# Head loads of a fused S5 and feed-forward kernel: equal halves on both queues, x cut by columns over all rows

## The chip, the cores and the metric

The kernel runs on one core of one Trainium2 chip. The metric is the device time of one execution in microseconds, the median of several runs. The engines of the core are TensorE (PE; its weight loads are PEld), VectorE (DVE), ScalarE (ACT), GpSimd (POOL) and SyncE (SP). SP and ACT issue DMAs, each on a queue of its own, and sixteen DMA engines serve both queues.

## The reference

One input x of shape [1, 2048, 448] in bfloat16 goes through two branches, which a gate mixes.

```python
x = A_x
g = _sigmoid((x * gate_w).sum(-1, keepdims=True))
a = _A_ref(x, Lambda_re, Lambda_im, B_re, B_im, C_re, C_im, log_dt, Dskip)
b = _B_ref(x, B_w1, B_w2)
return g * a + (1 - g) * b
```

Branch A is a diagonal complex state space: `Bu = x @ B_bar.T`, `h[t] = Lam_bar * h[t-1] + Bu[t]` over 2048 steps, `y = 2 * Re(h @ C.T) + x * Dskip`, with `dt = exp(log_dt)`, `Lam_bar = exp(dt * Lam)` and `B_bar = (Lam_bar - 1) / Lam * B`. Branch B is `silu(x @ w1) @ w2` with 1792 hidden columns. The input that B has under the name `B_x` isn't used: both branches take `A_x`.

## The kernel before

**Tiling.** Two successive time steps stand in one row: `x2` is [1024, 896], and columns 0-447 of it are the even steps, 448-895 the odd ones. TensorE needs x with its features on the partitions: `XT[:, j, :]` holds features 128j to 128j+127 of the even steps for j = 0 to 3, and of the odd steps for j = 4 to 7. The 448 features make three full row blocks and a remainder of 64 (j = 3), which shares TensorE with another remainder, one on the lower and one on the upper 64 partitions. `XR` holds the remainder on the other half of the partitions. `W1E[:, j, :]` is w1 in the same row blocks, its 1792 hidden columns cut into 14 blocks of 128, called fb.

**The order.** The program is written out by hand. A small tracker (class `Tracker`) turns the keys that each operation reads and writes into semaphore waits; the order on an engine is the order of the Python calls. An engine takes its instructions in that order, so what stands behind a waiting one waits too. The DMA issues of the ACT queue stand between ACT's own instructions.

**The head** is all that stands ahead of the first full feed-forward pair:

- Loads. The first 512 rows of `x2`, columns 0-511, come into `XH` as they are, in four row blocks k of 128 rows (SBUF partition p, block k). The first 768 columns of w1 come in row blocks j = 0, 1, 2. `XA` names the keys of the pieces of x. Before, SP loads: columns 0-255 of x block 0, half of the columns of W1 block 0, columns 0-383 of x block 2, all of W1 block 1, two small rows into `R` (log_dt and Lambda_re), columns 384-511 of x blocks 2 and 3. ACT loads: columns 0-255 of x block 1, the other half of W1 block 0, columns 0-383 of x block 3, columns 256-511 of x blocks 0 and 1, the row Lambda_im, all of W1 block 2. Behind these come, on both queues, the remainder of w1 (`ld_wr`) and the later columns (`ld_w3`). SP waits for the first remainder loads (`T.wait_all("sp", gE)`) ahead of its DMA transposes, which bring the rest of x, B and C.
- Transposes on TensorE. `turn_k(j, k)` (line 488) transposes a 128 x 128 block of `XH` into a PSUM bank; `turned_k` (line 498, 128 columns) and `turned_x` (line 504, 256 or 512 columns) copy it with VectorE into `XT`. `PB` gives the bank for each j.
- `ffn1_first` (line 430) is a generator: 24 matmuls for six hidden blocks over the first 512 rows, 12 for j = 0 with the rows in two halves h of 256 columns, then 6 each for j = 1 and j = 2 with 512 columns. `next(first)` runs it to its next `yield`, and transposes, copies and small work stand between.
- `rd` (line 463, VectorE) and `mm_cols` (line 469, TensorE) turn the three rows in `R` into columns (`PV`), from which VectorE and ACT make dt, the decay and the phases.
- `turned_x(3)` and the copy at line 568 write the remainder of x to `XT` and `XR`. `ffn1_rem` (line 444) adds the remainder matmuls, and the SiLU on ACT (line 452) empties two banks at a time. `warm` (line 478) issues matmuls on constants, the first 20 of them while the first loads are under way.

Behind the head the matmuls of line 362 (`lanes`) run, first the rest of the feed-forward for these 512 rows, then the others, the state space's `Bu`, the second feed-forward matmul (lines 811 and 796) and the output (line 1049).

Of the kernel before, what the change touches and what calls it, by code (L numbers as in the profile page):

```python
# [11 lines left out]
BF16 = DT.bfloat16  # L12
# [138 lines left out]
def gated_mix(nc, A_x, A_Lambda_re, A_Lambda_im, A_B_re, A_B_im, A_C_re, A_C_im, A_log_dt,  # L151
              A_Dskip, B_x, B_w1, B_w2, gate_w, out):
    with ExitStack() as ctx:
        E = ctx.enter_context
        T = Tracker(nc, ctx)

        def sb(name, shape, dtype):
            return E(nc.sbuf_tensor(name, list(shape), dtype))
# [4 lines left out]
        XT = sb("XT", [128, 8, NK], BF16)  # L163
        W1E = sb("W1E", [128, 4, F_FF], BF16)
# [6 lines left out]
        XR = sb("XR", [128, NK], BF16)  # L171
# [17 lines left out]
        ID = sb("ID", [128, 128], BF16)  # L189
# [31 lines left out]
        ps = E(nc.psum_tensor("ps", [128, 8, 512], F32))  # L221
# [3 lines left out]
        def ld(eng, dst, src, key, group=None):  # L225
            return T.dma(eng, lambda e: e.dma_start(dst, src), writes=[key], group=group)  # L226
# [5 lines left out]
        XE = [(["XTe000", "XTe001", "XTe010", "XTe011", "XTe02"], ["XTe03"]), (["XTe1"], ["XTer1"])]  # L232
        XO = [([f"XTo{h}"], [f"XTr{h}"]) for h in range(2)]

        def swap_xr(eng, h, odd):
# [18 lines left out]
        XA = ["XA0", "XA1", "XA2", "XA3", "XB0", "XB1"]  # L254
        FA, FB = 768, 1280
        x0 = x2[0:512, 0:512].rearrange("(k p) c -> p k c", p=128)

        def ld_w(eng, j, f0=0, f1=FA, key=""):
            ld(eng, W1E[:, j, f0:f1], B_w1[j * 128:(j + 1) * 128, f0:f1], f"W1Ej{j}{key}")

        def ld_row(eng, i, v):
            ld(eng, R[i:i + 1, 0:D], row(v), f"R{i}", gR if i < 2 else gR2)
# [9 lines left out]
                          B_w1[384:448, FA:].rearrange("p (n c f) -> p n c f", n=2, c=2)[:, :, c, :], f"W1Es{c}")  # L272
            return ld(eng, W1E[p, 3, 0:384], B_w1[384:448, 384 * c:384 * c + 384], f"W1Er{c}")

        for k, eng in enumerate(("sp", "act")):
            ld(eng, XH[:, k, 0:256], x0[:, k, 0:256], XA[k])
        for c, eng in enumerate(("sp", "act")):
            ld_w(eng, 0, 384 * c, 384 * c + 384, c)
        for k, eng in ((2, "sp"), (3, "act")):
            ld(eng, XH[:, k, 0:384], x0[:, k, 0:384], XA[k])  # L280
        ld_w("sp", 1)
        ld("act", XH[:, 0:2, 256:512], x0[:, 0:2, 256:512], XA[4])
        for i, (eng, v) in enumerate((("sp", A_log_dt), ("sp", A_Lambda_re), ("act", A_Lambda_im))):
            ld_row(eng, i, v)
        ld_w("act", 2)
        ld("sp", XH[:, 2:4, 384:512], x0[:, 2:4, 384:512], XA[5])
        T.op("act", lambda e: e.activation(JK[:, 0:1], HP[:, :], AF.Exp), reads=["HP"], writes=["JK0"])
        gE = [ld_wr(eng, c, False) for c, eng in enumerate(("sp", "act"))]
        ld_w3("sp", 0, 2, FA, FB, "d")
# [20 lines left out]
        for i, src in enumerate((A_B_re, A_B_im)):  # L310
# [15 lines left out]
             writes=["IOTA"])  # L326
# [9 lines left out]
        def nxt():  # L336
            n_bank[0] += 1
            return BANKS[(n_bank[0] - 1) % len(BANKS)]
# [58 lines left out]
        def ff(fb):  # L397
            i, c = fb // 2, fb % 2
            return i + 3 * c if i < 3 else i + 3 + 2 * c if i < 5 else i + 5 + 2 * c

        def wj(fb):
            i, c = fb // 2, fb % 2
            return [f"W1Ej0{c}", "W1Ej1", "W1Ej2"] if i < 3 else ["W1Ed0", "W1Ed2"] if i < 5 else ["W1Ee0", "W1Ee1"]
# [13 lines left out]
        def ffn1_pair(c, fb, p=None):  # L417
            odd, h = c // 2, c % 2
            banks = at(p) if p is not None else [nxt(), nxt()]
            return (*[(banks[i], odd, h, w1(fb + i)) for i in range(2)],  # L420
                    wj(fb) + wj(fb + 1) + (XO if odd else XE)[h][0], rem_ffn1(odd, h, fb),
                    lambda: ffn1_act(c, fb, banks[0], 2))

        def ffn1_first():
            banks = [nxt() for _ in range(NF1)]
            for j, h in ((0, 0), (0, 1), (1, None), (2, None)):
                c = slice(0, 512) if h is None else slice(256 * h, 256 * h + 256)
                for n, fb in enumerate((0, 2, 4, 1, 3, 5)):
                    bank = banks[fb]
                    T.op("pe", lambda pe, fb=fb, bank=bank, j=j, h=h, c=c: pe.matmul(  # L430
                        ps[:, bank, c], W1E[:, j, ff(fb) * 128:(ff(fb) + 1) * 128], XT[:, j, c],
                        start=(h == 0), stop=(h == 0), skip_group_check=(h != 0)),
                        reads=[f"W1Ej{j}" if j else f"W1Ej0{fb % 2}"] + (
                            ["XTe02"] if j == 2 else [f"XTe0{j}{h}"] if h is not None else [f"XTe0{j}0", f"XTe0{j}1"]),
                        writes=[f"ps{bank}"])
                    if (j, h, n) in ((0, 0, 3), (0, 0, 5), (1, None, 2), (1, None, 5)):
                        yield
            yield banks

# [34 lines left out]
        def warm(n, b):  # L474
            def mm(pe):
                ins = None
                for _ in range(n):
                    ins = pe.matmul(ps[:, b, 0:128], ones, ones, start=True, stop=True)
                return ins
            T.op("pe", mm, writes=[f"ps{b}"])  # L480

        warm(NWARM, 5)
        PB = (6, 7, 6, 7)
        xp = [ps[:, b, 0:256].bitcast(BF16) for b in PB]

        def turn_k(j, k, b=None):
            b = PB[j] if b is None else b
            T.op("pe", lambda pe: pe.transpose(  # L488
                ps[:, b, 0:256].bitcast(BF16)[:, k * 128:(k + 1) * 128], XH[:, k, j * 128:(j + 1) * 128], ID[:, :]),
                reads=[XA[k if j < 2 or (j == 2 and k > 1) else 4 + k // 2], "ID"], writes=[f"ps{b}"])  # L490

        def turn_x(j, i):
            for k in (2 * i, 2 * i + 1):
                turn_k(j, k)

        def turned_k(j, k, b):
            c = slice(128 * k, 128 * k + 128)
            T.op("dve", lambda e: e.tensor_copy(XT[:, j, c], ps[:, b, 0:256].bitcast(BF16)[:, c]),
                 reads=[f"ps{b}"], writes=[f"XTe0{j}{k // 2}" + ("" if k % 2 else "a")])

        def turned_x(j, i=None, b=None):
            c, key = (slice(0, 512), f"XTe0{j}") if i is None else (slice(256 * i, 256 * i + 256), f"XTe0{j}{i}")
            b = PB[j] if b is None else b
            T.op("dve", lambda e: e.tensor_copy(XT[:, j, c], ps[:, b, 0:256].bitcast(BF16)[:, c]),
                 reads=[f"ps{b}"], writes=[key])

        for k in range(2):
            turn_k(0, k, 6 - k)
            turned_k(0, k, 6 - k)
        turn_x(1, 0)  # L510
        turned_x(1, 0)
        warm(2, 4)
        first = ffn1_first()
        next(first)
        for k in (2, 3):
            turn_k(0, k, k + 4)
            turned_k(0, k, k + 4)
# [12 lines left out]
        turned_x(2)  # L530
        next(first)
        for i in range(2):
            turn_x(3, i)
# [24 lines left out]
        def pact(o, a, f, ra, scale=1.0, bias=0.0):  # L558
# [9 lines left out]
        T.op("dve", lambda e: e.tensor_copy(XR[64:128, 0:512], xp[3][0:64, :]), reads=["ps7"], writes=["XR0a"])  # L568
        T.op("act", lambda e: e.activation(JK[:, 0:1], HP[:, :], AF.Silu), reads=["HP"], writes=["JK0"])
        ld_b(GWB, gate_w, "GW")  # L570
        ld_b(DB, A_Dskip, "DB")
# [9 lines left out]
            reads=["f2"] + SGN, writes=["f2s"])  # L581
# [84 lines left out]
        for n in (32, 64):  # L666
            T.op("dve", lambda e, n=n: e.tensor_copy(GD[n:2 * n, :, :], GD[0:n, :, :]), reads=["GW", "DB"],
                 writes=["GW", "DB"])
# [7 lines left out]
             writes=["BTz"] + BTK[2:4])  # L676
# [174 lines left out]
        def bu_even(pt, h, p=None, q=None):  # L851
# [4 lines left out]
            def done():  # L856
# [14 lines left out]
        def bu3_even(p, q):  # L871
            b = at(p)

            def done():
# [288 lines left out]
        f = ffn1(2)  # L1163
# [100 lines left out]
```

## Time and profile before

| What | us |
|---|---|
| Median of 3 runs | 137.05 (136.32 to 137.05) |
| Span of the profiled execution | 135.2 |
| PE busy | 131.8 (97%) |
| DVE busy | 115.6 (86%) |
| ACT busy | 93.8 (69%) |
| POOL busy | 15.9 (12%) |

The span runs from the first instruction of the profiled execution to its last; a run's time holds what lies around it too. PE counts matmuls, PEld weight loads, which overlap them. The chain of waits follows the work that ended last back from its end, so its shares tell who sets the time. In a timeline or chain line the first number is the start and the second the length, both in us; what stands in brackets is the idle time of the engine ahead of it and who ended it. Two groups of the page show what the DMA queues carry in all (packets, MB, share of 16 engines): `q1` is SP's queue, `q10` ACT's.

```
q1 hardware_dynamic: 22996, 10.43, 33.4%
q10 hardware_dynamic: 1730, 1.20, 3.1%
```

### The profile page before, as it was taken

How to read it: one execution, taken by the hardware profiler on the slowest of the kernel's cores; microseconds unless marked ns; L12 is line 12 of the kernel's file. 1: busy time of each engine (PE TensorE's matmuls, PEld its weight loads, DVE VectorE, ACT ScalarE, POOL GpSimd, SP SyncE). 2: the span in 40 equal slices, each digit the busy share in tenths (PEclk: the TensorE clock that was granted, in tenths of full speed). 3: DMA queues.
4: the chain of work that ended last, by engine and by line, in shares of the span. 5: the costliest groups of instructions: out<-in, count | busy, mean ns of one | idle time of the engine just before them, and what ended most of it. 6: DMA issues, size and time to landing. Idle time of an engine off the chain costs nothing.

```text
span 135.2 us, 2632 instructions
## 1 busy us (share of the span) xinstructions
PE 131.8 (97%) x1072; PEld 65.4 (48%) x1073; DVE 115.6 (86%) x154; ACT 93.8 (69%) x146; POOL 15.9 (12%) x32
## 2 busy tenths in 40 slices
PE   7899999999999999999999999999999999999993
PEld 7444444444444554444445544445555555555552
DVE  1369999917899798999999999999999999994554
ACT  0459888899939999769999597797114437879200
POOL 7108349650000000000000000000000000000000
DMA  4999979898997220000222000000000000322123
GB/s 110 259 275 176 125 140 264 165 323 248 259 188 119 53 63 0 0 0 0 55 47 58 5 0 0 0 5 0 0 0 0 0 0 5 102 91 79 68 80 124
DMA packets 24736, 11.78 MB, mean 87 GB/s; under 512 B 16851, under 2 KB 24214, under 8 KB 24726
## 3 DMA queue, kind: packets, MB, share of 16 engines
q1 hardware_dynamic: 22996, 10.43, 33.4%
q10 hardware_dynamic: 1730, 1.20, 3.1%
q8 instruction: 8, 0.13, 0.4%
q14 instruction: 2, 0.02, 0.0%
HBM read 5.34 MB, written 1.84 MB: 53 GB/s over the span
## 4 chain that ended last, share of the span: by engine, by line
PE 94%; DMA 2%; DVE 1%; SPq 1%; issue 0%
PE ps L362 44%; PE ps L796 16%; PE ps L811 16%; PE ps L1049 15%; PE ps L430 3%; DMA XN<-in_A_x_dram 2%; PE ps L488 1%; DVE TMPS L1073 1%; SPq L226 1%; PE ps L444 1%; PE ps L469 0%
## 5 line engine op out<-in xcount | busy, mean ns | idle before, releaser
L362 PE MATMUL ps<-XT,W1E 64*128 64x512 bf16 x325 | 41.3, 376 | 0.0
L452 ACT ACTIVATE AT<-ps 128x1024 bf16<-128x1024 f32 x28 | 28.2, 1020 | 7.4 <-PE ps L362 7.2
L362 PEld LDWEIGHTS ps<-XT,W1E 64*128 64x128 bf16 x325 | 16.9, 94 | 19.1 <-ACT AT L452 0.3
L362 PE MATMUL ps<-XT,BT 64*128 64x512 bf16 x156 | 22.4, 376 | 0.0
L811 PE MATMUL ps<-W,AT 64*128 64x448 bf16 x224 | 21.5, 349 | 0.0
L796 PE MATMUL ps<-W,AT 128*128 128x448 bf16 x112 | 21.4, 353 | 0.0
L796 PEld LDWEIGHTS ps<-W,AT 128*128 128x128 bf16 x112 | 10.9, 98 | 10.5 <-issue 0.4
L811 PEld LDWEIGHTS ps<-W,AT 64*128 64x128 bf16 x224 | 10.9, 94 | 10.4
L840 ACT ACTIVATE BT<-ps,GT 128x448 bf16<-128x448 f32 x8 | 5.1, 634 | 13.2 <-PE ps L796 13.2
L896 DVE SCALAR_TENSOR_TENSOR HS<-VE,P,ps 128x512 bf16<-128x512 bf16 (+1 forms) x13 | 9.6, 781 | 3.8 <-PE ps L362 3.8
L362 PEld LDWEIGHTS ps<-XT,BT 64*128 64x128 bf16 x156 | 8.1, 94 | 9.4 <-DVE HS L896 0.4
L940 DVE TENSOR_TENSOR_SCAN G<-P,Q 128x1024 f32<-128x1024 f32 (+1 forms) x6 | 11.4, 1922 | 0.0
L1049 PE MATMUL ps<-CO,VE 128*128 128x448 bf16 (+2 forms) x63 | 11.1, 332 | 0.0
L1049 PE MATMUL ps<-CO,HS 128*128 128x448 bf16 x56 | 11.1, 352 | 0.0
L362 PE MATMUL ps<-XR,W1E 64*128 64x512 bf16 x25 | 9.2, 376 | 0.0
L1049 PEld LDWEIGHTS ps<-CO,VE 128*128 128x128 bf16 x63 | 6.0, 98 | 4.8
L1049 PEld LDWEIGHTS ps<-CO,HS 128*128 128x128 bf16 x56 | 5.5, 98 | 5.1
L893 DVE TENSOR_TENSOR Q<-G,COS 128x2048 bf16<-128x2048 f32 (+1 forms) x4 | 7.0, 1756 | 0.1
L893 DVE TENSOR_TENSOR Q<-G,SIN 128x2048 bf16<-128x2048 f32 (+1 forms) x4 | 7.0, 1752 | 0.0
L858 ACT ACTIVATE VE<-ps 128x1024 bf16<-128x1024 f32 x6 | 6.1, 1020 | 1.2 <-PE ps L362 1.2
L860 ACT ACTIVATE ps<-VE,P 128x1024 f32<-128x1024 bf16 x6 | 6.7, 1118 | 0.2
L896 DVE SCALAR_TENSOR_TENSOR VE<-HS,P,FP 128x512 bf16<-128x512 bf16 (+1 forms) x7 | 6.6, 977 | 0.1
(124 smaller groups left out, 181.0 us busy)
## 6 DMA issues: line engine op xcount, KB each, us to landing
W<-in_B_w_dram SPq DMA_DIRECT2D x2, 784.0 KB, 6.3
XN<-in_A_x_dram SPq DMA_DIRECT2D x1, 896.0 KB, 5.5
out_dram<-OT SPq DMA_DIRECT2D x8, 112.0 KB, 1.7
out_dram<-TMPS SPq DMA_DIRECT2D x7, 112.0 KB, 1.7
HS<-HS SPq DMA_DIRECT2D x4, 128.0 KB, 2.3
XN<-in_A_x_dram SPq DMA_DIRECT2D x1, 384.0 KB, 3.6
W1E<-in_B_w_dram SPq DMA_DIRECT2D x1, 256.0 KB, 5.6
W1E<-in_B_w_dram ACTq DMA_DIRECT2D x1, 256.0 KB, 5.6
```

Source lines behind the costliest of these rows:

```text
L362: ins = pe.matmul(ps[:, bank, :], w(p, j), xh(odd, h, j, p), start=start and j == js[0], stop=stop and j == js[-1], skip_group_check=seeded)
L430: T.op("pe", lambda pe, fb=fb, bank=bank, j=j, h=h, c=c: pe.matmul(ps[:, bank, c], W1E[:, j, ff(fb) * 128:(ff(fb) + 1) * 128], XT[:, j, c] ...
L452: T.op("act", lambda e: e.activation(a[:, fb:fb + n, :], ps[:, bank:bank + n, :], AF.Silu), reads=[f"ps{bank + i}" for i in range(n)], wri ...
L796: ins = pe.matmul(ps[:, bank, 0:D], a[:, fb, q * 128:(q + 1) * 128], W2[:, ff(fb), :], start=(first and fb == 0), stop=(fb == NFB - 1), sk ...
L811: ins = pe.matmul(ps[:, bank, 0:D], a[p, fb, q * 128:(q + 1) * 128], W2[p, ff(fb), :], start=(start and fb == 0), stop=(not start and fb = ...
L840: T.op("act", lambda e: e.activation(bs(tile), ps[:, bank, 0:D], AF.Copy, scale=sc), reads=[f"ps{bank}", "GT2" if h else "GRI"], writes=ks)
L858: T.op("act", lambda e: e.activation(VE[:, m:m + 2, hs], ps[:, b[0]:b[0] + 2, :], AF.Copy), reads=[f"ps{i}" for i in b], writes=vs)
L860: T.op("act", lambda e: e.activation(ps[:, o[0]:o[0] + 2, :], VE[:, m:m + 2, hs], AF.Copy, scale=c1("lr", pt)), reads=vs + ["lr"], writes= ...
L893: T.op("dve", lambda e: e.tensor_tensor(o, a, b, op), reads=reads, writes=writes)
L896: T.op("dve", lambda e: e.scalar_tensor_tensor(o, a, s, b, ALU.mult, ALU.add), reads=reads, writes=writes)
L940: T.op("dve", lambda e: e.tensor_tensor_scan(G[:, c, w], rb, Q1[:, c, w], init, ALU.mult, ALU.add), reads=[f"Q1{c}", "rr", f"G{c}"], write ...
L1049: ins = pe.matmul(ps[:, bank, c], state(kt, odd, m), CO[:, m, c], start=False, stop=(m == YB[-1]), skip_group_check=True)
```

## The change

Every load of the head is cut into two equal halves, one on each queue. x comes by columns 0-127, 128-255 and 256-511 of all 512 rows (SP takes row blocks 0 and 1, ACT 2 and 3), and each of these stands ahead of one W1 row block. W1 block 0 is cut by columns as before; blocks 1 and 2 are cut by rows, partitions 0-63 on SP and 64-127 on ACT. The three small rows move behind W1 block 2. On TensorE all four transposes of j = 0 come ahead of the first matmul, those of j = 1, 2 and 3 come four at a time, and `mm_cols` moves behind the transposes of j = 2 and three more matmuls. `turned_k` goes; VectorE's copies are two of 256 columns for j = 0 and one of 512 for each other j, and `rd` stands behind the copy of j = 2. The PSUM banks `PB` and the points at which `ffn1_first` yields are changed to suit, and one warm matmul is added.

```diff
-        for k, eng in enumerate(("sp", "act")):
-            ld(eng, XH[:, k, 0:256], x0[:, k, 0:256], XA[k])
-        for c, eng in enumerate(("sp", "act")):
+        HALVES = ((0, "sp"), (1, "act"))
+
+        def ld_x(n, c0, c1):
+            for i, eng in HALVES:
+                k = slice(2 * i, 2 * i + 2)
+                ld(eng, XH[:, k, c0:c1], x0[:, k, c0:c1], f"XA{n}{i}")
+
+        def ld_wh(j):
+            for i, eng in HALVES:
+                ld(eng, W1E[64 * i:64 * i + 64, j, 0:FA], B_w1[j * 128 + 64 * i:j * 128 + 64 * i + 64, 0:FA],
+                   f"W1Ej{j}{i}")
+
+        ld_x(0, 0, 128)
+        for c, eng in HALVES:
             ld_w(eng, 0, 384 * c, 384 * c + 384, c)
-        for k, eng in ((2, "sp"), (3, "act")):
-            ld(eng, XH[:, k, 0:384], x0[:, k, 0:384], XA[k])
-        ld_w("sp", 1)
-        ld("act", XH[:, 0:2, 256:512], x0[:, 0:2, 256:512], XA[4])
+        ld_x(1, 128, 256)
+        ld_wh(1)
+        ld_x(2, 256, 512)
+        ld_wh(2)
         for i, (eng, v) in enumerate((("sp", A_log_dt), ("sp", A_Lambda_re), ("act", A_Lambda_im))):
             ld_row(eng, i, v)
-        ld_w("act", 2)
-        ld("sp", XH[:, 2:4, 384:512], x0[:, 2:4, 384:512], XA[5])
...
-                    if (j, h, n) in ((0, 0, 3), (0, 0, 5), (1, None, 2), (1, None, 5)):
+                    if (j, h, n) in ((0, 1, 2), (1, None, 2), (1, None, 5), (2, None, 2)):
                         yield
...
-        PB = (6, 7, 6, 7)
+        PB = (6, 6, 7, 6)
...
-        for k in range(2):
-            turn_k(0, k, 6 - k)
-            turned_k(0, k, 6 - k)
-        turn_x(1, 0)
-        turned_x(1, 0)
-        warm(2, 4)
+        for i in range(2):
+            for k in (2 * i, 2 * i + 1):
+                turn_k(0, k, 6 + i)
+            turned_x(0, i, 6 + i)
+        warm(3, 4)
         first = ffn1_first()
         next(first)
-        for k in (2, 3):
-            turn_k(0, k, k + 4)
-            turned_k(0, k, k + 4)
+        for i in range(2):
+            turn_x(1, i)
+        turned_x(1)
         next(first)
-        for k in (2, 3):
-            turn_k(1, k, 6)
-        turned_x(1, 1, 6)
+        for i in range(2):
+            turn_x(2, i)
+        turned_x(2)
         rd()
         next(first)
         T.op("pe", mm_cols, reads=["R0", "R1", "R2", "Rd", "ID"], writes=["pv"])
...
-        for i in range(2):
-            turn_x(2, i)
-        turned_x(2)
         next(first)
         for i in range(2):
             turn_x(3, i)
```

What is left out are the keys: `XE`, `XA`, `wj` and the keys in `ffn1_first` and `turn_k` name the new pieces, and XR's copy reads bank 6.

More of the change, by code (lines that the diff above doesn't have):

```diff
@@ L230, in ldt @@
                          writes=[key, *also], group=group)
-        XE = [(["XTe000", "XTe001", "XTe010", "XTe011", "XTe02"], ["XTe03"]), (["XTe1"], ["XTer1"])]
+        XE = [(["XTe000", "XTe001", "XTe01", "XTe02"], ["XTe03"]), (["XTe1"], ["XTer1"])]
         XO = [([f"XTo{h}"], [f"XTr{h}"]) for h in range(2)]
@@ L253, in gated_mix @@
         XH = XN[:, 0:8 * D].rearrange("p (k c) -> p k c", k=4)
-        XA = ["XA0", "XA1", "XA2", "XA3", "XB0", "XB1"]
+        XA = [f"XA{n}{i}" for n in range(3) for i in range(2)]
         FA, FB = 768, 1280
@@ L402, in wj @@
             i, c = fb // 2, fb % 2
-            return [f"W1Ej0{c}", "W1Ej1", "W1Ej2"] if i < 3 else ["W1Ed0", "W1Ed2"] if i < 5 else ["W1Ee0", "W1Ee1"]
+            return [f"W1Ej{j}{c}" for j in range(3) for c in range(2)] if i < 3 else ["W1Ed0", "W1Ed2"] if i < 5 else ["W1Ee0", "W1Ee1"]
         def w1(fb):
@@ L432, in ffn1_first @@
                         start=(h == 0), stop=(h == 0), skip_group_check=(h != 0)),
-                        reads=[f"W1Ej{j}" if j else f"W1Ej0{fb % 2}"] + (
-                            ["XTe02"] if j == 2 else [f"XTe0{j}{h}"] if h is not None else [f"XTe0{j}0", f"XTe0{j}1"]),
+                        reads=[f"W1Ej{j}{i}" for i in (range(2) if j else (fb % 2,))] + [f"XTe0{j}" if h is None else f"XTe0{j}{h}"],
                         writes=[f"ps{bank}"])
-                    if (j, h, n) in ((0, 0, 3), (0, 0, 5), (1, None, 2), (1, None, 5)):
+                    if (j, h, n) in ((0, 1, 2), (1, None, 2), (1, None, 5), (2, None, 2)):
                         yield
@@ L489, in turn_k @@
                 ps[:, b, 0:256].bitcast(BF16)[:, k * 128:(k + 1) * 128], XH[:, k, j * 128:(j + 1) * 128], ID[:, :]),
-                reads=[XA[k if j < 2 or (j == 2 and k > 1) else 4 + k // 2], "ID"], writes=[f"ps{b}"])
+                reads=[f"XA{min(j, 2)}{k // 2}", "ID"], writes=[f"ps{b}"])
         def turn_x(j, i):
@@ L494, in turn_x @@
                 turn_k(j, k)
[L496 to L499, printed above, removed]
         def turned_x(j, i=None, b=None):
@@ L567, in gated_mix @@
         turned_x(3)
-        T.op("dve", lambda e: e.tensor_copy(XR[64:128, 0:512], xp[3][0:64, :]), reads=["ps7"], writes=["XR0a"])
+        T.op("dve", lambda e: e.tensor_copy(XR[64:128, 0:512], xp[3][0:64, :]), reads=["ps6"], writes=["XR0a"])
         T.op("act", lambda e: e.activation(JK[:, 0:1], HP[:, :], AF.Silu), reads=["HP"], writes=["JK0"])
```

## The prediction

> **What bounds the kernel now.** I read the chain of waits by line first. It says which engine sets the end.
>
> ```profile
> PE 94%; DMA 2%; DVE 1%; SPq 1%; issue 0%
> ...
> PE ps L362 44%; PE ps L796 16%; PE ps L811 16%; PE ps L1049 15%; PE ps L430 3%; DMA XN<-in_A_x_dram 2%; PE ps L488 1%; DVE TMPS L1073 1%; SPq L226 1%; PE ps L444 1%; PE ps L469 0%
> ```
>
> TensorE sets it, apart from the 2% of DMA and some issue time. The windows by stage (start:end, length, busy time of PE, PEld, DVE, ACT, POOL with counts, granted clock, DMA share, GB/s) show where PE is not busy.
>
> ```profile
> 0.00:10.53 10.53, 9.13 (x73) 5.92 (x76) 4.42 (x25) 3.78 (x7) 3.15 (x12) 1.00 0.82 211
> 10.53:42.29 31.76, 31.76 (x296) 14.14 (x294) 27.00 (x38) 27.14 (x33) 12.71 (x20) 1.00 0.97 207
> ```
>
> Behind 10.53 us PE has no gap, so a later or earlier end of the head moves the end of the kernel by as much. The chain in order of time gives the head, which is all that the change touches.
>
> ```profile
> 1.70 3.25 DMA XN<-in_A_x_dram
> 4.96 0.04 issue
> 5.00 0.39 PE ps L488 x2
> ...
> 9.78 0.75 PE ps L444 x6
> 10.53 31.76 PE ps L362 x294
> ```
>
> PE waits for x until 4.96 (0.53 us idle from 4.47) and then runs to the end. Last, the timeline of VectorE (start, length) at the end of the head:
>
> ```profile
> 8.52 0.42 DVE L504 COPY XT<-ps 128x512 bf16<-128x512 bf16 x1 [0.30 <-PE ps L488]
> 8.97 0.42 DVE L568 COPY XR<-ps 64x512 bf16<-64x512 bf16 x1
> ```
>
> The last two evictions end at 9.39. L444, which reads XR, starts at 9.71 because PE still has six matmuls of 0.216 us until 9.61. These evictions have 0.3 us of cover. This is the row that decides.
>
> **Transfers.** From the trace of before, issue and last landing, in us: x row blocks 0 and 1 at 0.78, landing 2.85 (SP) and 3.02 (ACT); W1 row block 0 at 1.24, landing 3.60 and 3.80; x row blocks 2 and 3 at 1.70, landing 4.96 and 5.12; W1 block 1 (SP) 6.42; x columns 256-511 of row blocks 0-1 (ACT) 6.66; W1 block 2 (ACT) 7.37; x columns 384-511 of row blocks 2-3 (SP) 7.57. Of the third and later pairs, 15 of 16 engines were done 0.6 to 0.8 us before the last one (third pair: 4.16 and 4.38). I take the late engine to stay.
>
> A packet takes 18 ns at 256 B, 27 at 512, 36 at 768, 65 at 1536 (medians of the packets before 12 us). x now goes as 512 + 512 packets of 256 B and 512 of 512 B: 32.3 us of engine time. Before it was 512 of 512 B, 256 of 768 and 256 of 256: 27.6. Over 16 engines that is 0.29 us more; W1 is the same bytes and packet sizes. Sums over 16 engines, in the order of the queues: before 0.43, 1.01, 1.58, 2.54, 3.34; after x1 0.58, W1-0 1.15, x2 1.73, W1-1 2.25, x3 3.11, W1-2 3.63. Shifting before's landings by the difference: x1 2.99 and 3.16, W1-0 3.74 and 3.94, x2 5.10 and 5.26, W1-1 6.25 (mean of 6.42 and 6.66, less 0.29), x3 7.24 (mean of 7.57 and 7.37, less 0.23), W1-2 7.76.
>
> The Trainium skill (DMA: Bandwidth & Descriptors, Specifications) puts line rate at 512 B and more, and a read-modify-write below. If a 256 B packet cost by that as much as a 512 B one, x1 and x2 would be 0.29 us longer each and the end some 0.6 us later. This trace's 18 against 27 ns speaks against so much.
>
> Each queue issues one DMA more ahead of the rest, some 0.42 us. The ACT table load (3.70) and the W1 remainder loads move by it. The remainder's packets start at 5.6 for an issue at 3.75, so the queue is backed up and hides it. Remainder landings go from 7.79 and 8.01 to about 8.3, L444 needs them at 9.7 or later; SP's transposes wait for the same landing and slip about 0.3. They meet VectorE work with 0.1 to 0.25 us to spare (XTr1 lands 27.30, its copy starts 27.45), but VectorE itself later idles 3.21 us for PE, so nothing is charged.
>
> **PE and VectorE, step by step.**
> - Start. All four transposes of j=0 precede the copies. Transposes at 3.05, 3.16, 3.22, 3.33; copy starts 0.35 after the last start (cold clock, as at 3.26 to 3.61), 0.29 each: 3.51-3.80 and 3.80-4.09. Two copies of 256 columns replace 128-column ones (0.29 for 2 x 0.225). First L430 0.15 after: 3.95 against 3.77. Nine matmuls, then 4.97.
> - Two edits are free: a third warm matmul (0.107) ends before the first copy does, at 3.8; and of the new banks (6, 6, 7, 6) each was evicted over 1 us before its next transposes, so no wait comes from them (0.3 to 0.4 us, one copy, if one did).
> - j=1. x2's halves at 5.10 and 5.26, PE idle about 0.15 (before 0.53). Last transpose starts 5.36, the three left of j=0 end 5.75. One 512-column copy starts 0.26 after the last transpose and takes 0.425: 6.04. W1-1 at 6.25, so j=1 starts 6.30, before 6.47: 0.17 gained. Three of them to 6.95.
> - j=2 transposes now need x3, 7.24: start 7.28, 0.33 idle. Before this data was there (7.23 start, PE-bound). Four at 0.055 to 0.065: 7.52; the other three of j=1 to 8.17; copy 7.71-8.13.
> - The small rows: R's three DMAs pass behind x3 and W1-2 on SP and ACT (landed 5.54 to 6.12, now some 7.1 to 7.8); `rd` stands behind the j=2 copy on VectorE: 8.13-8.30. `mm_cols` is next on PE: 8.36 to 8.46, 0.2 idle. Queued behind it are all matmuls of j=2.
> - j=2. Three matmuls 8.50-9.15, transposes of j=3 to 9.38 (last start 9.31), three more to 10.03. Before, six stood behind these transposes. Copies 9.57-9.99 and, for XR, 10.02-10.44. The cover of 0.3 us is gone: 0.65 us of matmul against 1.13 us from the last transpose to the end of XR. L444 at 10.50, 0.79 later than 9.71.
> - ACT. PV's copy, dt, ar, mag follow `mm_cols`: 8.81, 9.06, 9.30, 9.54; then a table load of 1.28 and JK: free at 11.03. The first SiLU would be ready 10.93 (0.43 after L444). Its end frees two banks for the second L362 pair, where PE and ACT were tied (ACT's end 11.16, PE 11.23). It adds 0.1: +0.9.
>
> Sum, by PE's starts. From the first L430 to L444 the work is the same: 12 matmuls of 0.109, 12 of 0.216, 12 transposes, `mm_cols` 0.10: 4.70 us. Before it took 9.71 - 3.77 = 5.94, so 1.24 of waits. After: x2 0.22 (0.17 and 0.05 for the second half), copy and W1-1 0.55, x3 0.33, `rd` 0.23, XR 0.47: 1.80. With the start 0.18 later that is +0.75 to 0.8, with ACT +0.9. Against the profiled span 135.2 that is 136.1; the timed median lies 1.85 above that span (137.05), so 137.95, say 137.9. The runs spread from 136.32.
>
> **Bounds.** Lower: all DMAs land with the 15th engine (x2 4.52, W1-1 5.6, x3 6.5). Then waits vanish, but the one wide copy of j=1 (5.40-5.82), three matmuls per stop, and the XR tail remain: j=1 5.88, j=2 transposes 6.55, `mm_cols` 7.62, j=3 transposes 8.40, XR 9.69, L444 9.75: +0.05, with ACT +0.15. If copies and first matmul were also as early as before, about -0.2. So this head can't gain 1% (1.37 us); a run of before differs from another by half a percent, and 1% is about what a measurement can tell from no change.
>
> **Rivals.**
> 1. The landings run at the 15-engine pace. For: the late engine's gap is one event near 3.1 to 4.9 us that may not recur. Against: every landing from then to 10 us shows it. 137.05 + 0.15 = 137.2.
> 2. The 64-partition halves run slowly. W1-1 and W1-2 go as two loads of 64 partitions each. If the two took turns at half the engines' rate, each block would take 1.04 instead of 0.52 us: W1-1 6.77, x3 7.76, W1-2 8.80. By the steps above: j=1 6.82, j=2 transposes 7.80, R at about 8.5, `mm_cols` 8.88, j=2 9.00, XR 10.94, L444 11.0, +1.3, with ACT +1.4: 138.45. With 0.3 more from R it is 138.75. It decides from an extra 0.4 us per block on. Against: the remainder loads of W1 are 64-partition halves on the two queues already, and their packets take the common 36 ns, with a few of 170 to 570 at first touch. For: no 64-partition load there stands alone on the engines.
> 3. The change gains what it wants: x2 and x3 are there, evictions as early as before: 136.85.
>
> The Trainium skill has a rule for rival 2 (DMA: Bandwidth & Descriptors, Rules for kernel authors): two transfers to disjoint partition halves serialize, one of 128 partitions is better; SBUF — State Buffer, Door 1, measures 196 against 328 GB/s for 64 and 128 partitions. By that, rival 2. The trace's 36 ns packets do not agree so far.
>
> **How the numbers follow.** Forecast +0.9, chance 0.45; rival 1 0.2; rival 2 0.25; rival 3 0.1. The forecast is the likeliest case, 137.9. The range takes in rival 3's and rival 2's ends: 136.8 to 138.9. Slower by over 1% (above 138.42): rival 2 with 0.22, and 0.09 of the forecast's upper side (R or x3 0.5 later): 0.31. Faster by over 1% (below 135.68): nothing in the head gives it, 0.05 for what I don't see. Within 1%: 0.64.
>
> **What would show it.** In the profile after: first L430 matmul at 3.95; idle of PE before the transposes of j=2 for DMA x, about 0.3; `mm_cols` after a wait for `rd`; PE idle 0.4 before L444's line, which starts at 10.5 behind the XR copy, and the chain passing through that copy; no other gap behind. Wrong if W1-1 lands past 6.7 (rival 2), or if x3 lands before 6.9 and L444's line starts before 9.9 (rival 1 or 3), or if PE has new gaps past 11 us.

## The result and the profile after

The changed kernel takes 138.0 us (median of four runs, 137.55 to 138.04); the kernel before, in four runs, 136.81 (136.32 to 137.05). The ratio is 1.0084, 95% interval 1.0058 to 1.0111: slower, by about 0.8%. The profiled spans are 136.5 and 135.2 us.

A span is listed to 0.1 us for every timed execution too. Over six executions of the changed kernel, those of the experiments below included, the mean is 136.23, over 50 later executions of before 135.15, so 1.08 us of the loss lies in the span. What lies outside it grew from 1.47 to 1.56. Together that is 1.17 us. One more execution of before, at 138.52 us, ran in a slower state and is left out.

The page of the kernel after, the chain of waits by engine and by line:

```profile
PE 96%; DVE 2%; issue 0%
PE ps L371 43%; PE ps L795 16%; PE ps L810 16%; PE ps L1048 15%; PE ps L439 3%; PE ps L486 2%; PE ps L496 1%; DVE TMPS L1072 1%; DVE XT L507 1%; PE ps L452 1%; DVE XR L567 0%; PE ps L477 0%
```

L439 and L452 are the two kinds of FFN1 matmul of the head (L430 and L444 before), L496 the transposes, L486 the warm matmuls, L507 and L567 the copies out of PSUM. The 2% of "DMA XN" is gone, and so is SP's queue. In their place stand L486, two copies of L507 and the XR copy: the chain no longer waits for x, but for TensorE and VectorE in turn.

The windows by stage, in the columns given for before. The boundary stands at 11.90, which is 0.14 us behind the start of the L371 matmuls in the chain below; for before it stood right at the start of that stage:

```profile
0.00:11.90 11.90, 10.48 (x77) 6.89 (x79) 4.02 (x22) 3.77 (x7) 3.16 (x12) 1.00 0.78 200
11.90:43.60 31.70, 31.70 (x298) 14.09 (x295) 27.06 (x38) 27.08 (x33) 12.73 (x20) 1.00 0.94 206
```

The stage behind the head is again all PE, without a gap. The head is what grew, and it moves less data per microsecond (200 GB/s against 211).

The chain of the kernel after in order of time (start, length, what):

```profile
3.95 2.02 PE ps L439 x9
5.97 0.44 PE ps L496 x4
6.44 0.43 DVE XT L507
...
7.01 0.81 PE ps L439 x3
...
8.72 0.24 PE ps L477 x4
8.96 0.69 PE ps L439 x3
9.65 0.24 PE ps L496 x4
...
9.91 0.42 DVE XT L507
...
10.37 0.43 DVE XR L567
10.80 0.14 issue
10.93 0.82 PE ps L452 x6
11.76 31.80 PE ps L371 x294
```

Two things are to be seen. At the bottom, the tail that the prediction describes: transposes of j = 3 at 9.65, then two copies in a row on VectorE, and L452, which reads XR, behind them. At the top, something that it does not have: nine matmuls of 256 columns take 2.02 us. They stand 0.213 us apart; in before, from 4.1 us on, the same matmul stands at 0.109. The granted clock of the window is 1.00 all the while.

VectorE's timeline at the end of the head, kernel after:

```profile
9.91 0.42 DVE L507 COPY XT<-ps 128x512 bf16<-128x512 bf16 x1 [0.15 <-PE ps L496]
10.37 0.42 DVE L567 COPY XR<-ps 64x512 bf16<-64x512 bf16 x1
```

Before, these two copies ended at 9.39 and PE had matmuls until 9.61. Now they end at 10.79, and PE's last matmul of j = 2 has ended 0.41 us before L452 starts. L452 starts at 10.93 against 9.71, which is 1.22 later; the span is 1.27 longer. From the start of that line to the end of the span it is 125.57 us now and 125.52 before: whatever the change did, it did ahead of that line. In what follows "the remainder line" is L444 or L452, by kernel, and its start is the gauge.

### The profile page after: what moved, and what is told of

It reads as the page before. It is cut to its first block, busy times and chain, and to the rows that moved or that the text cites. A ratio compares the mean times of both kernels' runs of the same rounds, so it can differ in the third digit from the quotient of the medians.

```text
span 136.5 us, 2633 instructions
## 1 busy us (share of the span) xinstructions
PE 133.0 (97%) x1074; PEld 66.3 (49%) x1074; DVE 115.2 (84%) x151; ACT 93.7 (69%) x146; POOL 15.9 (12%) x32
## 3 DMA queue, kind: packets, MB, share of 16 engines
q1 hardware_dynamic: 23268, 10.47, 32.4%
q10 hardware_dynamic: 2002, 1.17, 3.0%
## 4 chain that ended last, share of the span: by engine, by line
PE 96%; DVE 2%; issue 0%
PE ps L371 43%; PE ps L795 16%; PE ps L810 16%; PE ps L1048 15%; PE ps L439 3%; PE ps L486 2%; PE ps L496 1%; DVE TMPS L1072 1%; DVE XT L507 1%; PE ps L452 1%; DVE XR L567 0%; PE ps L477 0%
## 5 line engine op out<-in xcount | busy, mean ns | idle before, releaser
L371 PE MATMUL ps<-XT,W1E 64*128 64x512 bf16 x325 | 41.4, 376 | 0.0
L460 ACT ACTIVATE AT<-ps 128x1024 bf16<-128x1024 f32 x28 | 28.2, 1019 | 7.3 <-PE ps L371 7.2
L371 PEld LDWEIGHTS ps<-XT,W1E 64*128 64x128 bf16 x325 | 16.9, 94 | 19.0 <-ACT AT L460 0.4
L371 PE MATMUL ps<-XT,BT 64*128 64x512 bf16 x156 | 22.4, 376 | 0.0
L371 PEld LDWEIGHTS ps<-XT,BT 64*128 64x128 bf16 x156 | 8.1, 94 | 9.4 <-DVE HS L895 0.3
L371 PE MATMUL ps<-XR,W1E 64*128 64x512 bf16 x25 | 9.2, 376 | 0.0
L507 DVE COPY XT<-ps 128x512 bf16<-128x512 bf16 (+1 forms) x5 | 1.8, 371 | 5.9 <-PE ps L496 5.9
```

The source lines that it names most:

```text
L371: ins = pe.matmul(ps[:, bank, :], w(p, j), xh(odd, h, j, p), start=start and j == js[0], stop=stop and j == js[-1], skip_group_check=seeded)
L460: T.op("act", lambda e: e.activation(a[:, fb:fb + n, :], ps[:, bank:bank + n, :], AF.Silu), reads=[f"ps{bank + i}" for i in range(n)], wri ...
```

## The experiments

Two theories stood after the first profile. **Order:** the loss is made by two moves in the order of work. The small rows' DMAs stand behind W1 block 2, so `rd` and `mm_cols` are late, and the transposes of j = 3 stand behind three more matmuls of j = 2, so the XR copy loses its cover. **Halves:** W1's row blocks, cut into loads of 64 partitions, arrive later than whole ones. A third came up from the slow matmuls above: **rate**, that TensorE runs at half its rate until some moment, and that the changed kernel feels this more.

### Both kernels once more

Each unchanged, profiled a second and a third time on other chips.

> The kernel before, unchanged, for a second profile. Theory T (tail order): the first remainder matmul starts at 9.7 plus or minus 0.2 us whenever TensorE reaches its full rate (256-column matmuls going from 0.213 to 0.109 us apart), because PE waits for x anyway. Rival C (the late full rate is chance and is what the change lost): the full rate comes at a time that differs from execution to execution, and where it comes at 6 us or later this kernel too starts its remainder matmuls 0.5 us or more later.

> The changed kernel, unchanged, for a second profile. T: remainder matmuls again start 1.0 to 1.3 us later than in the kernel before, about 0.4 us of it idle time on VectorE's copy of XR, at whatever time the full rate comes. C: if the full rate comes near 4 us here, they start at 10.2 or earlier (0.5 us later than before at most).

> The kernel before, unchanged, for a third profile. T: first matmul of j=1 at 6.2 to 6.6 and remainder matmuls at 9.6 to 9.9, even if TensorE stays at half rate past 5.5 us, because half of its work on j=0 stands behind the wait for x. C: 0.5 us later if the full rate comes past 5.5 us.

> The changed kernel, unchanged, for a third profile. T with the part of the clock that e2_after_look showed: remainder matmuls at 10.3 to 10.5 if the full rate comes before 4.5 us, at 10.7 to 11.0 if it comes past 5.5 us; 0.4 us idle on XR's copy in either case.

| profile | 256-column matmuls at 0.109 from | start of remainder line | span |
|---|---|---|---|
| before, first | 4.1 | 9.71 | 135.23 |
| before, second | 4.2 | 9.66 | 135.18 |
| before, third | about 5.7 | 9.74 | 135.25 |
| after, first | about 6.4 | 10.93 | 136.50 |
| after, second | 3.9 or earlier | 10.35 | 135.91 |
| after, third | about 5.2 | 10.47 | 136.03 |

PE's timeline in the second profile of the kernel after (start, length, line, count; in brackets idle time before it and what ended it):

```profile
3.90 1.15 PE L439 MATMUL ps<-XT,W1E 128*128 128x256 bf16 x9
4.89 0.39 PE L496 MATMUL ps<-ID,XN 128*128 128x128 bf16 x4
...
6.37 0.81 PE L439 MATMUL ps<-XT,W1E 128*128 128x512 bf16 x3 [0.77 <-DMA W1E<-in_B_w_dram]
...
10.35 0.37 PE L452 MATMUL ps<-XT,W1E 64*128 64x512 bf16 x1 [0.41 <-DVE XR L567]
```

Here the nine matmuls take 1.15 us, as the prediction assumed. PE is done early and waits 0.77 us for W1 block 1, starts j = 1 at 6.37 where it was 7.01, and reaches the remainder 0.58 us earlier than in the first profile. The XR wait is 0.41 us in both. The 10.35 is 0.69 later than the second profile of before: less than the 1.0 to 1.3 that the order theory expected, more than the 0.5 that its rival allowed. Now the third profile of the kernel before:

```profile
4.25 1.04 PE L430 MATMUL ps<-XT,W1E 128*128 128x256 bf16 x4 [0.38 <-DMA W1E<-in_B_w_dram]
...
8.35 1.46 PE L430 MATMUL ps<-XT,W1E 128*128 128x512 bf16 x6
9.74 0.39 PE L444 MATMUL ps<-XT,W1E 64*128 64x512 bf16 x1
```

Four matmuls take 1.04 us here, so the full rate came late in this execution too, and the remainder starts only 0.03 to 0.08 later than in the other two. In before, PE's slow part lies where it waits for x and W1 anyway. In the kernel after the late full rate is enough to give the 0.58 us between its first and second profile, since the copy behind the slow matmuls released j = 1 there. It was not alone: W1 block 1 also landed later, at 6.66 against 6.28, so at the full rate j = 1 would still have started only at about 6.75. The moment of the full rate does not explain why the changed kernel is slower: in its best profile it is still 0.61 us behind the worst of before (10.35 against 9.74). Nor is it shown to make the spread of the timed executions: before hardly moved with it, and its spans spread from 134.7 to 135.7.

### Order: both moves undone, in the changed kernel

All other parts of the change stay. The rows are issued ahead of x's third part, `rd` and `mm_cols` come ahead of j = 2's transposes, and the transposes of j = 3 come ahead of all six matmuls of j = 2. The fourth bank becomes 7, and XR's copy reads it.

```diff
         ld_wh(1)
-        ld_x(2, 256, 512)
-        ld_wh(2)
         for i, (eng, v) in enumerate((("sp", A_log_dt), ("sp", A_Lambda_re), ("act", A_Lambda_im))):
             ld_row(eng, i, v)
+        ld_x(2, 256, 512)
+        ld_wh(2)
...
-                    if (j, h, n) in ((0, 1, 2), (1, None, 2), (1, None, 5), (2, None, 2)):
+                    if (j, h, n) in ((0, 1, 2), (1, None, 2), (1, None, 5)):
...
-        PB = (6, 6, 7, 6)
+        PB = (6, 6, 6, 7)
...
         turned_x(1)
-        next(first)
-        for i in range(2):
-            turn_x(2, i)
-        turned_x(2)
         rd()
         next(first)
         T.op("pe", mm_cols, reads=["R0", "R1", "R2", "Rd", "ID"], writes=["pv"])
...
+        for i in range(2):
+            turn_x(2, i)
+        turned_x(2)
         next(first)
         for i in range(2):
             turn_x(3, i)
```

> The changed kernel with the loads of the change, but the end of the head in the order of before: the three small rows behind W1 block 1, rd and mm_cols ahead of the transposes of j=2, and the transposes of j=3 ahead of all six matmuls of j=2. T: remainder matmuls at about 10.2 instead of 10.9, no idle time on XR's copy, time 0.6 to 0.8 us less than the changed kernel (about 137.3, ratio to before 1.003 to 1.005). C: the order of the tail doesn't matter, ratio to before 1.007 to 1.01 as for the change unless the full rate comes early. D (the 64-partition halves and smaller packets of x are what is late): the remainder matmuls stay at 10.7 or later, with PE idle on DMA in place of VectorE.

136.93 us, ratio 1.0030 (1.0014 to 1.0045): as the order theory expected, at the lower edge of its range; the remainder came earlier than expected (9.75 against 10.2). PE's timeline:

```profile
6.02 0.81 PE L439 MATMUL ps<-XT,W1E 128*128 128x512 bf16 x3 [0.28 <-DVE R L471]
...
7.17 0.49 PE L496 MATMUL ps<-ID,XN 128*128 128x128 bf16 x4 [0.26 <-DMA XN<-in_A_x_dram]
...
8.14 0.39 PE L496 MATMUL ps<-ID,XN 128*128 128x128 bf16 x4
8.36 1.46 PE L439 MATMUL ps<-XT,W1E 128*128 128x512 bf16 x6
9.75 0.39 PE L452 MATMUL ps<-XT,W1E 64*128 64x512 bf16 x1
```

The second group of transposes is j = 3's, at 8.14, followed by six matmuls as in before. The remainder starts at 9.75 with no wait in brackets: the XR copy has its cover again. Undoing the two moves takes back 0.0084 - 0.0030 = 0.0054 of the loss, about 0.74 us, with the loads cut as the change cuts them. Not all of that is TensorE's order. W1 block 1 came earlier too: its later half landed at 5.67 to 5.82 in the three kernels with the small rows right behind it, and at 6.17 to 6.66 in the five profiles of kernels with x3 there, which fits its having the DMA engines to itself for longer; j = 1 starts at 6.02. And the move has its own price: two row DMAs on SP ahead of x3 push x3's issue from 2.89 to 3.78, and j = 2's transposes wait 0.26 us for it. (The 0.28 us at 6.02 is j = 1's copy; `rd`, put down there, lies behind that copy on VectorE.)

### Order: one of the moves, put into the kernel before

The transposes of j = 3 are put behind three matmuls of j = 2, and nothing else is changed.

```diff
-                    if (j, h, n) in ((0, 0, 3), (0, 0, 5), (1, None, 2), (1, None, 5)):
+                    if (j, h, n) in ((0, 0, 3), (0, 0, 5), (1, None, 2), (1, None, 5), (2, None, 2)):
...
         turned_x(2)
         next(first)
+        next(first)
         for i in range(2):
             turn_x(3, i)
```

> The kernel before with one edit: three of the six matmuls of j=2 go ahead of the transposes of j=3. T: the 0.3 us of cover is lost here too, remainder matmuls start about 0.4 us later than in the kernel before (10.1 to 10.2), ratio 1.002 to 1.004. C and D: no loads and no clock are touched, so no change (ratio 0.999 to 1.001).

137.21 us, ratio 1.0041 (1.0023 to 1.0059): the mean span grows from 135.11 to 135.72. PE's timeline:

```profile
8.99 0.39 PE L488 MATMUL ps<-ID,XN 128*128 128x128 bf16 x4
9.21 0.81 PE L430 MATMUL ps<-XT,W1E 128*128 128x512 bf16 x3
10.43 0.37 PE L444 MATMUL ps<-XT,W1E 64*128 64x512 bf16 x1 [0.41 <-DVE XR L569]
```

The 0.41 us wait of the changed kernel appears in before, by this one move. The ratio is just above what was expected; the remainder is later than expected (10.43 against 10.1 to 10.2). A second, smaller wait comes with the move: the first matmul of j = 2 stands 0.34 us behind the last of j = 1 instead of 0.216, because the transposes no longer cover the copy of j = 2. In this execution the 256-column matmuls came to the full rate only at about 6.0 us.

### Order: each move undone alone, in the changed kernel

First only the rows, `rd` and `mm_cols` come early, with the loads and banks of the kernel with both moves undone; the transposes of j = 3 stay behind three matmuls of j = 2:

```diff
-                    if (j, h, n) in ((0, 1, 2), (1, None, 2), (1, None, 5)):
+                    if (j, h, n) in ((0, 1, 2), (1, None, 2), (1, None, 5), (2, None, 2)):
...
         turned_x(2)
         next(first)
+        next(first)
         for i in range(2):
             turn_x(3, i)
```

This diff is against the kernel with both moves undone. The other half, against the changed kernel, lets the transposes of j = 3 follow `mm_cols` directly, and leaves the rows late:

```diff
-                    if (j, h, n) in ((0, 1, 2), (1, None, 2), (1, None, 5), (2, None, 2)):
+                    if (j, h, n) in ((0, 1, 2), (1, None, 2), (1, None, 5)):
...
-        next(first)
         for i in range(2):
             turn_x(3, i)
```

> The changed kernel with the first half of that order alone: the three small rows behind W1 block 1, rd and mm_cols ahead of the transposes of j=2; the transposes of j=3 stay behind three of the six matmuls of j=2. T: the wait of mm_cols for rd (0.1 to 0.2 us) goes, the 0.4 us idle on XR's copy stays; ratio to before 1.005 to 1.008. Rival: the small rows were the whole loss, then 1.003 as with both.

> The changed kernel with the second half alone: the transposes of j=3 behind mm_cols and ahead of all six matmuls of j=2; rows, rd and mm_cols stay late. T: VectorE now reaches the last two copies late, because PV's copy and the two operations that follow it stand ahead of them and hang on the late mm_cols; the idle time on XR shrinks to 0.2 to 0.35 us; ratio 1.005 to 1.008. Rival: the place of these transposes was the whole loss, then 1.003 and no idle time on XR.

Rows alone: 137.55 us, 1.0075 (1.0053 to 1.0096). Transposes alone: 137.73, 1.0087 (1.0065 to 1.0109), a little above what was expected. Each alone gives nothing that can be measured against 1.0084; both together gave 0.0054. They do not add: seen from the kernel with both moves undone (1.0030), either move put back costs nearly the whole, 0.0057 for the late rows and 0.0045 for the late transposes. Each profile shows what takes the gain. Rows alone, PE's timeline:

```profile
8.42 0.81 PE L439 MATMUL ps<-XT,W1E 128*128 128x512 bf16 x3 [0.41 <-DMA W1E<-in_B_w_dram]
...
10.51 0.37 PE L452 MATMUL ps<-XT,W1E 64*128 64x512 bf16 x1 [0.41 <-DVE XR L567]
```

The XR wait stays, as it should, and a new wait of 0.41 us for W1 block 2 stands where the wait for `rd` was: behind the row DMAs that block was issued at 4.32 and landed at 8.33. Transposes alone, first PE's timeline, then ACT's:

```profile
10.33 0.37 PE L452 MATMUL ps<-XT,W1E 64*128 64x512 bf16 x1 [0.19 <-DVE XR L566]
```

```profile
9.66 1.28 ACT L567 ACT_TABLE_LOAD   x1
10.95 0.20 ACT L567 ACTIVATE JK<-HP 128x1 bf16<-128x1 f32 x1
11.06 1.92 ACT L460 ACTIVATE AT<-ps 128x1024 bf16<-128x1024 f32 x2
```

The XR wait halves to 0.19, and the remainder starts at 10.33. But with `mm_cols` still late, ACT's small steps and its table load are late, and the first SiLU (L460) starts at 11.06, 0.73 us behind the remainder's start, where before has 0.43 and the changed kernel 0.49. PE's matmuls that need the banks which this SiLU empties start 0.48 us behind the ones ahead of them (11.64 to 12.12), against 0.24 in the changed kernel (12.24 to 12.48). Behind the remainder this kernel is the only one that loses: 125.81 us from its start to the end of the span against 125.5 to 125.6 in all others.

### Halves: whole W1 row blocks in the changed kernel

```diff
-        ld_wh(1)
+        ld_w("sp", 1)
         ld_x(2, 256, 512)
-        ld_wh(2)
+        ld_w("act", 2)
```

The matmuls' keys name the whole blocks; nothing else differs.

> The changed kernel with W1 blocks 1 and 2 each as one load of 128 partitions, block 1 on SP and block 2 on ACT; x by columns and the order on the engines stay. T: W1 block 1 lands within 0.3 us of the changed kernel's two looks (6.3 to 6.7), the remainder matmuls start within 0.3 us of theirs, ratio 1.006 to 1.011. D (two halves of 64 partitions are slower): block 1 lands by 5.7 and the ratio is 1.005 or less.

137.84 us, 1.0096 (1.0076 to 1.0117), not faster than with halves. PE's timeline:

```profile
6.36 0.82 PE L439 MATMUL ps<-XT,W1E 128*128 128x512 bf16 x3 [0.54 <-DMA W1E<-in_B_w_dram]
...
7.47 0.40 PE L496 MATMUL ps<-ID,XN 128*128 128x128 bf16 x4 [0.29 <-DMA XN<-in_A_x_dram]
...
10.75 0.37 PE L452 MATMUL ps<-XT,W1E 64*128 64x512 bf16 x1 [0.41 <-DVE XR L567]
```

Block 1 as one load of 192 KB landed at 6.32, and j = 1 started at 6.36. As two halves, ahead of x3 as here, the later one landed at 6.17 to 6.66. The price of rival 2 was 0.52 us for each block and it decided from 0.4 on; the mean of the halves (6.40) and the whole (6.32) differ by less than the profiles with halves among themselves, and the kernel with whole blocks is no faster. So the halves are not seen to be what the changed kernel lost by. The landings alone would not settle it, since beside the whole block the other queue carried half of x3, and a lower rate of halves is not excluded: from 4 to 5 us the DMA engines moved 158 GB/s in the changed kernel and 192 with whole blocks (240 in before).

The Trainium skill (DMA: Bandwidth & Descriptors, Rules for kernel authors) says that two transfers to disjoint partition halves serialize, as they share the same engines, and advises one transfer of 128 partitions. Landings this close agree that the halves gain nothing. By that rule alone a pair of halves is not slower than a whole block either, so rival 2, which the prediction takes from it, needs more than the rule; no run here shows that extra cost.

A whole block is worse for x: with 192 KB on one queue ahead of it, x3's later half landed at 7.43 (7.06 to 7.35 in the four profiles with x3 right behind the halves and the rows behind W1 block 2), and the transposes of j = 2 wait 0.29 us.

### A better place for the rows

Both moves undone, but the rows behind x3 and ahead of W1 block 2, so that x3 is not held up. `mm_cols` comes behind the transposes of j = 2, PV's copy ahead of the copy of j = 2. Against the changed kernel:

```diff
         ld_x(2, 256, 512)
-        ld_wh(2)
         for i, (eng, v) in enumerate((("sp", A_log_dt), ("sp", A_Lambda_re), ("act", A_Lambda_im))):
             ld_row(eng, i, v)
+        ld_wh(2)
...
         turned_x(1)
+        rd()
         next(first)
         for i in range(2):
             turn_x(2, i)
-        turned_x(2)
-        rd()
-        next(first)
         T.op("pe", mm_cols, reads=["R0", "R1", "R2", "Rd", "ID"], writes=["pv"])
...
+        turned_x(2)
         next(first)
         for i in range(2):
             turn_x(3, i)
```

The yield at `(2, None, 2)` goes and the fourth bank is 7, as above.

> The loads of the change with the three small rows behind the third piece of x, mm_cols behind the transposes of j=2 and PV's copy ahead of theirs, the transposes of j=3 ahead of all six matmuls of j=2. T: x's third piece is issued 0.9 us earlier than in e3_rows_t3_early, so PE's 0.26 us wait for it shrinks and the remainder matmuls start at 9.5 to 9.7; ratio to before 0.998 to 1.002. If the loads themselves still cost: 1.003 as with e3_rows_t3_early.

137.39 us, 1.0061 (1.0042 to 1.0080), outside what was expected, and the remainder starts at 10.14 instead of 9.5 to 9.7. The idea was to keep the gain of both moves without the price. PE's timeline:

```profile
7.95 0.59 PE L439 MATMUL ps<-XT,W1E 128*128 128x512 bf16 x2
...
8.75 1.46 PE L439 MATMUL ps<-XT,W1E 128*128 128x512 bf16 x6
10.14 0.39 PE L452 MATMUL ps<-XT,W1E 64*128 64x512 bf16 x1
```

There is no XR wait, but the six matmuls of j = 2 start at 8.75 where they started at 8.36. W1 block 2 was issued at 4.20 and 4.39 behind the rows and landed at 8.49 and 8.66. `rd` waited 0.79 us for the rows, the last of which landed at 7.24. The price moved from x3 to W1 block 2 and to the rows themselves.

### What is left with both moves undone

The transposes of j = 1 come behind six of the twelve matmuls of j = 0 instead of nine, so that the wide copy behind them has six matmuls beside it instead of three. Against the kernel with both moves undone:

```diff
-                    if (j, h, n) in ((0, 1, 2), (1, None, 2), (1, None, 5)):
+                    if (j, h, n) in ((0, 0, 5), (1, None, 2), (1, None, 5)):
```

> e3_rows_t3_early with one more edit: the transposes of j=1 behind six matmuls of j=0 instead of nine, so that six and not three of them stand between these transposes and the first matmul of j=1. T: the copy of j=1 (0.28 us idle in e3_rows_t3_early, 0.15 in the changed kernel) is covered at either rate of TensorE, so the first matmul of j=1 waits for nothing but W1 block 1 and starts by 6.2 us at the full rate and by 6.9 at half rate; ratio to before 0.999 to 1.002. Rival D (loads): no change against e3_rows_t3_early, 1.003.

136.96 us, 1.0023 (1.0008 to 1.0039), just above what was expected and the same as without this edit (1.0030, 1.0014 to 1.0045). PE's timeline:

```profile
5.78 1.58 PE L439 MATMUL ps<-XT,W1E 128*128 128x256 bf16 x9
...
9.78 0.39 PE L452 MATMUL ps<-XT,W1E 64*128 64x512 bf16 x1
```

The nine matmuls in one group, six of 256 columns and three of 512, show that PE no longer waits for j = 1's copy, although the full rate came only at about 5.7 us. The remainder starts at 9.78 and the profiled span is 135.3, within 0.1 us of before. The timed executions are not: mean span 135.47 against 135.24 for before on the same chip, and for the kernel with both moves undone 135.41 against 135.11. So 0.2 to 0.3 us remain in the span of an average execution, and a little under 0.1 outside it. One profiled execution of each does not show where they lie, and j = 1's copy is not all of it. A result that does not differ from the one without this edit is also what rival D expected, by which the loads as the change cuts them still cost something. No run has whole blocks together with both moves undone, so D is neither shown nor excluded, and the rest stays open. No version was faster than the kernel before.

## Why the prediction was right, and where its steps were not

The forecast was +0.9 us and 137.9; measured were +1.17 and 138.0. That the median comes so close is in part luck, since two things offset each other: the base of 137.05 was high (50 later executions of before have a mean of 136.6), and the increase was some 0.3 too small. The 1.85 us that the prediction puts outside the span come from that base; the same 50 executions show 1.47.

The forecast's steps against the first profile, and against the second profile of the same kernel, in which the full rate came early:

| step | forecast | first profile | second profile |
|---|---|---|---|
| first L439 matmul | 3.95 | 3.89 | 3.90 |
| transposes of j = 1 | 5.14 | 5.77 | 4.89 |
| start of j = 1 | 6.30 | 7.01 | 6.37 |
| transposes of j = 2 | 7.28 | 7.65 | 7.02 |
| `mm_cols` | 8.36 | 8.72 | 8.14 |
| transposes of j = 3 | 9.15 | 9.49 | 8.91 |
| remainder line | 10.50 | 10.93 | 10.35 |

- **XR's lost cover: right.** The wait was put at 0.47 and is 0.41 us. The same move alone costs before 0.0041. This is the row that the prediction said decides.
- **`rd` and `mm_cols`: right.** 0.23 forecast, 0.20 measured (`rd` ends at 8.58, PE's first `mm_cols` matmul at 8.72). That undoing this alone gives nothing is not in the prediction: the rows change places with W1 block 2, for which PE then waits 0.41.
- **"12 matmuls of 0.109": the step that failed.** The sum charges the 256-column matmuls at the full rate from the first on, though its own sentence on the first copies already spoke of a "cold clock". In the first profile they stood 0.213 apart, and the nine took 1.87 us instead of the 0.98 charged; the four transposes ahead of j = 1's copy run slow as well (0.107 apart against 0.056). The transposes start only 0.63 late, since the wait for x that was charged is gone. Then the copy, not W1 block 1, releases j = 1 (7.01 against 6.30), and the later steps carry 0.34 to 0.43 of it to the end. Behind the copy a second error was hidden: W1 block 1 landed at 6.66, not 6.25, so j = 1 could not have started before about 6.75 at the full rate either. In the second profile, with the early rate and a landing at 6.28, the remainder starts at 10.35, 0.15 before the forecast.
- **x2's late engine: wrong.** The prediction took the sixteenth engine's delay to stay, and x2's landing to be 5.10 and 5.26. It landed at 4.19 and 4.46, and in the later profiles of before the same pair of loads landed at 4.4 to 4.8 instead of 4.96 and 5.12. A late sixteenth engine is not gone, but it does not stay with a load: in the first profile of the changed kernel it shows on W1 block 1 (fifteenth engines at 5.89 and 6.14, the last at 6.43 and 6.66), in the second hardly (6.00 and 6.22, then 6.08 and 6.28). So rival 1 was right for x2 (4.52), not for W1 block 1 (5.6) or x3 (6.5). It did not get its time: the earlier x2 let PE into a chain that did not wait for x.
- **x3: landing right, wait gone.** 7.24 forecast, 6.91 and 7.26 measured. The 0.33 us wait for it did not show in the first profile: PE came only at 7.65.
- **The queues: issue later than charged.** One more DMA on each queue was put at 0.42 us; the first remainder loads of W1 were issued at 4.94 and 5.15 instead of 3.75 and 3.77. They landed at 8.17 and 8.37, as forecast (8.3), and no new gap came of it.
- **ACT: small, as forecast.** +0.1 for the first SiLU behind the table load; from the remainder's start to the end 0.05 us was lost. The experiment with the transposes alone shows the size that it has when PE gets ahead of it: some 0.3.
- **Rival 2, slow halves, 138.45: not borne out.** W1 block 1 came at 6.66, near its 6.77, but x3 at 7.26 and W1 block 2 at 7.85, where it has 7.76 and 8.80; and whole blocks are no faster. That the first time lay between the forecast and rival 2 would have made it easy to believe.
- **Rival 3, the gain: not seen.** x did come in time. W1 block 1 did not always: PE waited 0.77 us for it in the second profile. And the order of work behind them spends more than a gain there could give.

Of the 1.08 us in the span, the two moves of order, W1 block 1's later landing among them, make some 0.8 (136.23 with them against 135.41 and 135.47 without, on a base of before that differs by 0.1 between the chips), and 0.2 to 0.3 stays unplaced.

## What to carry to other kernels

A load order that brings every operand in time gains nothing if the last eviction ahead of the next phase moves behind the matmuls that covered it: count the matmuls that stand between the last transpose and the first reader of its copy. A tiny row DMA costs its queue about as much issue time as a large load (0.47 and 0.33 us for rows of 0.9 KB ahead of x3, 0.41 for the 128 KB of x3 on that queue), so its place decides what comes late, and moving it moves the wait. Before a sum prices the first matmuls of a kernel, look at their spacing there, not at the same matmul later on.

## What was not expected of the hardware

The moment from which 256-column matmuls stand 0.109 instead of 0.213 us apart differed between executions of one program: 3.9 us or earlier, about 5.2 and about 6.4 in three profiles of the kernel after, 4.1, 4.2 and about 5.7 in three of the kernel before, with warm matmuls from 0.82 on in all six. The granted clock in the profile reads 1.00 throughout, so it does not show this; the spacing does. The Trainium skill (TensorE: Matmul & The Clock Gate, Part 1) describes a half rate at the start that ends after a busy window of some 3.4 us which runs free of the kernel's start; the factor of 0.213 to 0.109 agrees, and a moment that moves from run to run does too, over a wider span than the half microsecond either way that the page gives.

Two row DMAs of 0.9 KB ahead of x3 held its issue on SP back by 0.89 us (2.89 to 3.78).

The time outside the span was 1.47 us for before, 1.56 for the changed kernel, and 1.40 for the same kernel with W1's blocks whole (six executions). What makes that difference was not tried.
